# First expert layer of a fused attention and two-expert kernel: h of all tokens first, then y by seven products

## The chip, the core and the metric

One core of a Trainium2 chip. The metric is the device time of one launch in microseconds; the kernel before takes 979.49 us (median of three runs, 979.18 to 980.4). TensorE does matmuls into PSUM (eight banks of 512 float32 columns), VectorE, ScalarE and GpSimd work on elements, and all DMAs of this kernel are issued by SyncE's queue (SP).

## The reference

Everything is float32. Attention over 4 batches, 8 heads, 576 tokens, 64 channels, with a mask by blocks of 64 tokens; its output is 2304 tokens of 512 channels. Two expert layers follow:

```
x = attention(q, k, v)                      # scores only where block(query) >= block(key)
x = x.transpose(0, 2, 1, 3).reshape(2304, 512)
h = x @ moe_w_in                            # 512 x 2048
g = where(h >= 1, h, where(h <= -1, 0, (h + 1)**2 / 4))
x = g @ moe_w_out                           # 2048 x 512
h = x @ moe2_w_in
out = maximum(0.01 * h, h) @ moe2_w_out
```

The weights arrive as 64-bit floats; a conversion on the chip makes float32 of them.

## The kernel before

**Split operands.** Every operand of an expert matmul is split into a high and a low part that TensorE takes at full rate (float32r), and each product is three matmuls: high x high, low x high, high x low. One matmul contracts 128 rows and streams its columns past 128 loaded weight columns.

**Attention.** Sixteen pairs of heads, each in two units: `a` (tokens 0 to 319 of a batch) and `b` (320 to 575). A unit has scores (`unit_scores`, L555 for the plain form, L559 for the split one), softmax on VectorE, ScalarE and GpSimd (L466 to L486: maximum, exponential with sum, reciprocal, scaling of the probabilities on GpSimd), transposes on TensorE (L647), their copies out (L652, L654), values (L663), a split of the result (L676, L678) and a store to the DRAM tensor `x1d`. Its buffers are two "rooms" in the SBUF slots P1 and P2; it uses two PSUM slots of two banks, three for the first four units.

**First expert layer.** `moe_block` runs for blocks of tokens: five of 256, two of 512. For each pair of 128-row groups (`fc`) of w_in it makes h (L730), then on ScalarE and VectorE g and its two parts gh and gl (L738 to L744), and then at once the share of y (L761) that these rows of g give; y stays in two PSUM banks (four for the 512 blocks) until the block ends, and goes to the DRAM tensor `x2d` (L783). TensorE alternates h, y and attention. All of w_in and w_out of this layer lies in 16 SBUF tiles `w0` to `w15`.

**Conversions.** `w_float`, `w_hi` and `w_lo` convert the 32 halves of w1 at the start (L405 to L419, L374, L382). `conv_unit` converts w2 in 32 units and forms the seven combinations of weight blocks that the second layer takes (L810 to L823), and stores them to `wcd`; that runs beside the two 512 blocks.

**Second expert layer.** In two phases: h of all tokens (`h_step`, L937), stored to DRAM (`gd`), then y (`y_unit`, L1002) in units of 256 positions. Both use seven products in place of eight on matrices cut into 2x2 blocks (`PRODUCTS`, `ORDER`); tokens are paired as position (first half of a batch, second half). `sums` (L846, L848) adds the seven results up to four blocks, `w_load` brings the combined weights back and splits them (L833 to L835), `y_unit` loads g, forms its differences (L983) and splits them (L988 to L992).

**Order.** A planner (`Plan`) lists every operation with an engine, a cost, a priority and its reads and writes, simulates a list schedule in which each engine takes the waiting operation of lowest priority number, and emits the instructions in that order; each engine's queue on the chip then runs in that fixed order. The constants T_ and AHEAD set the priorities. A DMA counts as an operation of SP. Until the first h matmul, and between y matmuls of block 0, gaps of TensorE in the plan are filled with matmuls of zeros (`fill`).

Of the kernel before, what the change touches and what calls it, by code (L numbers as in the profile page):

```python
# [32 lines left out]
BLOCKS = [(256 * i, 256) for i in range(5)] + [(1280, 512), (1792, 512)]  # L33
# [11 lines left out]
W1_LO = ("dve", "pool")  # L45
W2_LO = ("dve", "pool")
T_MOE, T_FIRST, T_BLOCK, T_CONV = 30.0, 66.0, 66.0, 4.4
A1_LATE, A1_STEP, T_PACE = 0.0, 10.0, 2.4

AHEAD = 30.0  # L50
# [67 lines left out]
class Slot:  # L118
# [7 lines left out]
    def begin(self, dtype):  # L126
        self.n += 1
        n = self.n
        self.dtype = dtype
        self.live = []  # L130
        self.era = Buf(self.plan, ("slot", self.name), 1, lambda: self.pool.tile(
            [128, self.size], dtype, tag=self.name, name=f"{self.name}_{n}", bufs=1))
# [122 lines left out]
def fused_kernel(ctx, tc, qk, qk2, v, w1, w2, out):  # L255
# [84 lines left out]
    phase = {"late": False}  # L340

    def bank(i):

        ar = None if i in (4, 5) else ps_d if phase["late"] else ps_c
        return Bank(plan, (i,), lambda: banks[i], ar)

    def xbuf(i, tb):


        if tb < 384:  # L350
            where = ((A0, A1)[i % 2], 0), ((A0, A1)[i % 2], 1024)
        else:
            where = ((P1, 0), (P1, 2048)) if i == 5 else ((A0, 0), (A1, 0))
        for sl_ in dict.fromkeys(w[0] for w in where):
            sl_.begin(F32R)
        return [w[0].reg(w[1], NKC * tb, shape=lambda ap: ap.rearrange("p (k t) -> p k t", k=NKC)) for w in where], where[0][0]
# [11 lines left out]
    def w_tile(layer, fc):  # L368
        W[layer, fc] = pt(wp, [128, 2, 1024], F32R, f"w{fc}", f"w{layer}_{fc}", 1)

    def w_hi(prio, layer, fc, half, src, view, sb):
        t = W[layer, fc]
        s = slice(half * 512, half * 512 + 512)
        act(512, prio, lambda: nc.scalar.activation(t.get()[:, 0, s], view(), AF.Copy), [src],  # L374
            [(t, (half * 2, half * 2 + 1))], sb=sb)

    def w_lo(prio, layer, fc, half, src, view, sb, eng="dve"):
        t = W[layer, fc]
        s = slice(half * 512, half * 512 + 512)

        def f():
            (nc.vector if eng == "dve" else nc.gpsimd).tensor_tensor(  # L382
                t.get()[:, 1, s], view(), bc(t.get()[:, 0, s]), op=ALU.subtract)
        rw = [src, (t, (half * 2, half * 2 + 1))], [(t, (half * 2 + 1, half * 2 + 2))]
        if eng == "dve":
            dve(512, prio, f, *rw, port=sb)
        else:
            plan.op("POOL", 1225, prio, f, *rw, True)

    def w_float(prio, layer, fc, half, hs, keep=None, raw=None, sg=None):  # L390
# [3 lines left out]
        n = f"{layer}_{fc}_{half}"  # L394
        raw = raw or wraw()
        sg = sg or wsg()
        src = w1[fc, :, half * 1024:half * 1024 + 1024]
# [14 lines left out]
        part = None  # L412
        if keep is None:
            dst, view = hs, hs.get
        elif keep == "sg":
            dst, view = sg, sg.get
        else:
            dst, view, part = keep, lambda: keep.get()[:, half * 512:half * 512 + 512], (half, half + 1)
# [755 lines left out]
```

## Time and profile before

| | us |
|---|---|
| median of three runs | 979.49 |
| the profiled execution | 981.28 |
| span of its profile | 979.5 |
| TensorE busy | 959.4 (98%) |
| VectorE busy | 661.6 (68%) |
| ScalarE busy | 511.9 (52%) |
| GpSimd busy | 269.0 (27%) |
| DMA | 158.40 MB, mean 162 GB/s |

The span runs from the first to the last instruction of the program on the profiled execution; PE is TensorE's matmuls, PEld its weight loads, DVE VectorE, ACT ScalarE, POOL GpSimd, SPq SyncE's queue. The record of a matmul includes its way through the array, so that consecutive matmuls overlap: the price of one is taken from the length of a run in the chain of waits, divided by its count. The clock is TensorE's granted one as a share of 2.4 GHz. The DMA share is the mean busy share of the core's 16 DMA engines. The stages: attention and conversions until about 125 us, attention beside the 256 blocks until about 430, the 512 blocks until about 614, then the second layer's h until about 791 and its y until the end.

### The profile page before, as it was taken

Reading aid. Unit: us, or ns where it says so; the run is one execution under the profiler, and the core shown is the slowest. Engines: PE = TensorE matmul, PEld = TensorE weight load, DVE = VectorE, ACT = ScalarE, POOL = GpSimd, SP = SyncE. Lnnn points to the kernel's source line nnn. Section 1 sums busy time; section 2 is a strip of 40 time slices with the busy share of each in tenths; the row PEclk is TensorE's granted clock in tenths of the full one; section 3 lists DMA queues with packets and bytes.
Section 4 is the critical chain, followed back from the end, with each engine's and each line's share of the span. In section 5 each row is a group of like instructions: output and inputs, shape, how many; then the busy total and the mean of one; then the engine's idle time right before and its main releaser. Section 6 shows DMA issues by size and latency. Waiting matters only on the chain.

```text
span 979.5 us, 18953 instructions
## 1 busy us (share of the span) xinstructions
PE 959.4 (98%) x7040; PEld 878.5 (90%) x7040; DVE 661.6 (68%) x1229; ACT 511.9 (52%) x1064; POOL 269.0 (27%) x490
## 2 busy tenths in 40 slices
PE   8789999999999999999999999999999999999997
PEld 6578889889899899998888888999999999999997
DVE  4988855665655556545656754666757999988876
ACT  5677865666565566544444654342334654334332
POOL 6666533223241221336776410202020000000000
PEclk9999999999999999999999999999999999999999
DMA  7666542434425223488677732533434983443523
GB/s 242 196 213 216 177 161 74 158 96 130 150 84 157 84 73 106 130 273 293 224 261 242 284 104 76 189 119 134 136 122 146 302 279 105 144 137 116 148 80 109
DMA packets 113469, 158.40 MB, mean 162 GB/s; under 512 B 11232, under 2 KB 91104, under 8 KB 113376
## 3 DMA queue, kind: packets, MB, share of 16 engines
q1 hardware_dynamic: 113376, 157.19, 49.9%
q8 instruction: 55, 0.90, 0.4%
q14 instruction: 38, 0.31, 0.1%
HBM read 105.78 MB, written 51.38 MB: 160 GB/s over the span
## 4 chain that ended last, share of the span: by engine, by line
PE 91%; DVE 3%; ACT 2%; DMA 2%; issue 1%; POOL 0%; SPq 0%; DVEq 0%; ACTq 0%
PE bank L730 21%; PE bank L761 20%; PE bank L937 18%; PE bank L1002 17%; PE slot L647 5%; PE slot L663 5%; PE slot L559 2%; PE slot L555 2%; ACT rp L475 1%; DMA wraw<-w 1%; DMA gd<-ra 0%; DMA rg<-gd 0%; POOL rp L486 0%; DVE w L382 0%; DVE nmb L468 0%
## 5 line engine op out<-in xcount | busy, mean ns | idle before, releaser
L761 PE MATMUL bank<-rg,w 128*128 128x256 f32 (+1 forms) x1344 | 223.4, 316 | 0.0
L761 PEld LDWEIGHTS bank<-rg,w 128*128 128x128 f32 x1344 | 191.5, 188 | 21.6 <-issue 4.6
L730 PE MATMUL bank<-ra,w 128*128 128x256 f32 (+1 forms) x1152 | 180.7, 305 | 2.1 <-DVE rg L744 1.3
L937 PEld LDWEIGHTS bank<-rp,wc 128*128 128x128 f32 x1344 | 179.5, 189 | 1.0 <-ACT ra L848 0.7
L937 PE MATMUL bank<-rp,wc 128*128 128x288 f32 x1344 | 179.9, 296 | 0.5 <-ACT ra L848 0.5
L730 PEld LDWEIGHTS bank<-ra,w 128*128 128x128 f32 x1152 | 156.8, 189 | 17.9 <-issue 6.5
L1002 PE MATMUL bank<-wc,rp 128*128 128x256 f32 x1014 | 150.7, 282 | 0.8 <-DVE rp L990 0.8
L1002 PEld LDWEIGHTS bank<-wc,rp 128*128 128x128 f32 x1014 | 133.8, 188 | 1.0 <-DVE rp L990 1.0
L846 DVE TENSOR_TENSOR ra<-bank,ra 128x288 f32<-128x288 f32 (+2 forms) x203 | 93.1, 486 | 41.7 <-ACT ra L848 22.9
L741 DVE SCALAR_TENSOR_TENSOR bank<-bank,g 128x512 f32<-128x512 f32 x72 | 50.1, 696 | 69.4 <-ACT g L740 69.2
L738 ACT ACTIVATE g<-bank 128x512 f32<-128x512 f32 x72 | 42.9, 596 | 71.6 <-PE bank L730 71.4
L821 POOL TENSOR_TENSOR rp<-rp 128x128 f32<-128x128 f32 x128 | 67.5, 552 | 36.2 <-DVE rp L817 34.2
L486 POOL TENSOR_SCALAR rp<-rp,rsb 128x448 f32<-128x448 f32 (+1 forms) x64 | 47.7, 755 | 105.3 <-DVE rsb L481 100.5
L647 PE MATMUL slot<-ident,rp 128*128 128x128 f32 x480 | 64.8, 281 | 7.3 <-POOL rp L486 4.8
L744 DVE TENSOR_TENSOR rg<-bank,rg 128x512 fp32r<-128x512 f32 x72 | 49.5, 688 | 27.1 <-ACT rg L743 26.6
L743 ACT ACTIVATE rg<-bank 128x512 fp32r<-128x512 f32 x72 | 43.0, 597 | 41.1 <-DVE bank L741 41.1
L486 POOL TENSOR_SCALAR rp<-rp,rsa 64x64 f32<-64x64 f32 (+2 forms) x96 | 40.9, 441 | 85.7 <-DVE rsa L481 85.6
L647 PEld LDWEIGHTS slot<-ident,rp 128*128 128x128 f32 x480 | 55.2, 144 | 10.2 <-POOL rp L486 5.9
L989 ACT ACTIVATE rp<-ra 128x1024 fp32r<-128x1024 f32 (+1 forms) x39 | 37.8, 969 | 45.3 <-DVE ra L983 38.7
L1002 PE MATMUL bank<-wc,wraw 128*128 128x256 f32 x294 | 60.4, 282 | 0.2 <-DVE wraw L990 0.2
L941 ACT ACTIVATE ra<-ra 128x1152 f32<-128x1152 f32 x24 | 28.0, 1167 | 58.0 <-DVE ra L846 58.0
L663 PE MATMUL slot<-rp,rp 128*64 128x256 f32 (+2 forms) x512 | 57.2, 366 | 0.0
(122 smaller groups left out, 1424.2 us busy)
## 6 DMA issues: line engine op xcount, KB each, us to landing
wraw<-w SPq DMA_DIRECT2D x64, 256.0 KB, 3.7
wcd<-rp SPq DMA_DIRECT2D x32, 448.0 KB, 3.0
wc<-wcd SPq DMA_DIRECT2D x32, 448.0 KB, 4.2
gd<-ra SPq DMA_DIRECT2D x24, 576.0 KB, 3.6
wraw<-w SPq DMA_DIRECT2D x22, 512.0 KB, 4.2
rp<-qk SPq DMA_DIRECT2D x16, 416.0 KB, 3.2
rp<-gd SPq DMA_DIRECT2D x52, 128.0 KB, 2.9
rp<-gd SPq DMA_DIRECT2D x23, 256.0 KB, 3.2
```

The lines of the kernel that those rows point to most:

```text
L486: pool(keys, prio, lambda probs=probs, k=k, i=i, rows=rows: nc.gpsimd.tensor_scalar(probs[k]()[0:rows], probs[k]()[0:rows], rs.get()[0:row ...
L647: nc.tensor.transpose(s.get()[:, hd, o:o + 128], pr.get()[:, hd, a:a + 128], ident.get())
L663: nc.tensor.matmul(s.get()[64 * hd:64 * hd + 64, 0, q0:q0 + m], lhsT=vt.get()[:, j, 64 * hd:64 * hd + 64], rhs=pts[i].get()[:, hd, o:o + m ...
L730: nc.tensor.matmul(ps.get()[:, j * tb:(j + 1) * tb], lhsT=win(0, fc, p, kc), rhs=xt[x].get()[:, kc], start=(k == 0 and kc == 0 and j == 0) ...
L741: dve(nw, pv, lambda ps=ps, gt=gt: nc.vector.scalar_tensor_tensor(ps.get()[:, 0:nw], ps.get()[:, 0:nw], 1.0, gt.get()[:, 0:nw], op0=ALU.ma ...
L743: act(nw, pv, lambda ps=ps, gh=gh: nc.scalar.activation(gh.get()[:, 0:nw], ps.get()[:, 0:nw], AF.Copy), [ps], [gh])
L744: dve(nw, pv, lambda ps=ps, gh=gh, gl=gl: nc.vector.tensor_tensor(gl.get()[:, 0:nw], ps.get()[:, 0:nw], bc(gh.get()[:, 0:nw]), op=ALU.subt ...
L761: nc.tensor.matmul(y[o].get()[:, e * tb:(e + 1) * tb], lhsT=wout(0, fc, p)[:, ec * 128:ec * 128 + 128], rhs=x.get()[:, j * tb:(j + 1) * tb ...
L821: plan.op("POOL", 430, prio, lambda o=o, a=a, b=b, op=op: nc.gpsimd.tensor_tensor(sl(o), sl(a), sl(b), op=op), [(fx, (a, a + 1)), (fx, (b, ...
L846: dve(cols, prio, lambda: nc.vector.tensor_tensor(out(o), P[b][1](), out(a), op=ALU.add), [P[b][0], (slots, (a, a + 1))], [(slots, (o, o + ...
L937: nc.tensor.matmul(ps.get()[:, 0:HALF], lhsT=wc(0, p, cw, li, 128 * kc, 128 * kc + 128), rhs=r.get()[:, cx, kc], start=(k == 0 and kc == 0 ...
L1002: nc.tensor.matmul(ps.get()[:, 256 * t:256 * t + 256], lhsT=x.get()[:, n * zi + 128 * t:n * zi + 128 * t + 128], rhs=wc(1, p, cw, li, 0, 2 ...
```

## The change

The first layer gets the form of the second. `h1_block` makes h and g of nine blocks of 256 tokens, beside the attention, and stores g to DRAM (`gd[0]`); `y_unit` is made general and makes y of all positions after that, with seven products, in units of 232 positions (the last has 224) where the weights are the loaded operand and g streams. Positions now pair the tokens of two blocks of 256 (`runs`), within the first block two halves of 128. Only w_in of w1 is converted at the start (`w_float`, sixteen times, into `w0` to `w7`); w_out of w1 goes through `conv_unit` into `wcd`, as w2 does, and the conversion of w2's second half moves into the second layer's h. The tiles `w8` to `w15` are free until y begins, and hold three more rooms for the attention, the raw words of `w_float`, and the buffers of the 32 conversions that run beside the attention. The attention has three PSUM slots throughout (banks 0 to 3, 6 and 7; h has 4 and 5), and up to two units of scores ahead of the values. The order of its units is written out, b and a of the next batch in turn, and `NEED` says how many units precede each block. The filler ends with the first h matmul.

```diff
-BLOCKS = [(256 * i, 256) for i in range(5)] + [(1280, 512), (1792, 512)]
+NBLK = 9
...
-T_MOE, T_FIRST, T_BLOCK, T_CONV = 30.0, 66.0, 66.0, 4.4
-A1_LATE, A1_STEP, T_PACE = 0.0, 10.0, 2.4
-
-AHEAD = 30.0
+SQUARE = ("act",)
+T_MOE, T_FIRST, T_BLOCK, T_CONV = 30.0, 50.0, 41.0, 2.8
+T_UNIT = 10.2
+DEPTH = 2
+T_W2, T_NEXT = 100.0, 7.0
+
+AHEAD = 45.0
...
+    C = {i: Slot(plan, wp, f"w{i}", 1792) for i in range(8, NFC)}
...
+    ROOMS = {0: {"p": [(P1, 0)], "v": (P2, 1536), "qk": (P2, 2560)},
+             1: {"p": [(P2, 0)], "v": (P2, 2176), "qk": (P2, 3392)},
+             2: {"p": [(C[8], 0), (C[9], 0)], "v": (C[8], 1152), "qk": (C[10], 0)},
+             3: {"p": [(C[11], 0)], "v": (C[12], 0), "qk": (C[12], 384)},
+             4: {"p": [(C[13], 0), (C[14], 0)], "v": (C[13], 1152), "qk": (C[15], 0)}}
...
+    def h1_block(i, p0, dp, hbanks):
+
+        xt = XB[i]
+        for p in range(NP2):
...
+                for k, (c, x) in enumerate(((0, 0), (1, 0), (0, 1))):
+                    def f(fc=fc, j=j, k=k, c=c, x=x, ps=ps):
+                        plan.fill = None
+                        for kc in range(NKC):
+                            nc.tensor.matmul(ps.get()[:, j * 256:(j + 1) * 256], lhsT=win(fc, c, kc),
+                                             rhs=xt[x].get()[:, kc], start=(k == 0 and kc == 0 and j == 0),
+                                             stop=(k == 2 and kc == NKC - 1), skip_group_check=True)
+                    pe(4 * 119.5, pr + 0.01 * j, f, [(W[p], (2 * c + j, 2 * c + j + 1)), xt[x]], [ps])
+            gt = G2.reg(turn("g1", (0, 512, 1024, 1536)), 512)
+            pv = pr - 8
+            act(512, pv, lambda ps=ps, gt=gt: nc.scalar.activation(gt.get(), ps.get(), AF.Relu, bias=0.5, scale=0.5), [ps], [gt])
...
+                act(512, pv, lambda gt=gt: nc.scalar.activation(gt.get(), gt.get(), AF.Square), [gt], [gt], sb=True)
+            dve(512, pv, lambda ps=ps, gt=gt: nc.vector.scalar_tensor_tensor(
+                gt.get(), ps.get(), 1.0, gt.get(), op0=ALU.max, op1=ALU.min), [ps, gt], [gt])
...
+            dma(262144, pv + 1, lambda src=src, dst=dst: nc.sync.dma_start(dst, src()), [gt], where)
...
     def h_step(b, p, pr, dp, banks_):
-        h = (turn("h", (A0, A1, G2)) if b < B - 1 else (A1, A0)[p % 2]).reg(0, 1152, shape=lambda ap: ap.rearrange("p (s t) -> p s t", s=4))
+        h = (A1, A0)[p % 2].reg(0, 1152, shape=lambda ap: ap.rearrange("p (s t) -> p s t", s=4))
...
                     def f(k=k, cw=cw, x=x[0] if isinstance(x, tuple) else x, ps=ps, li=li, zi=zi, p=p):
                         for t in range(nt):
-                            nc.tensor.matmul(ps.get()[:, 256 * t:256 * t + 256],
-                                             lhsT=x.get()[:, n * zi + 128 * t:n * zi + 128 * t + 128],
-                                             rhs=wc(1, p, cw, li, 0, 256), start=(p == 0 and k == 0 and t == 0),
-                                             stop=(p == NP2 - 1 and k == 2), skip_group_check=True)
+                            a, e = (0, n) if wide else (128 * t, 128 * t + 128)
+                            b = wc(z, p, cw, li, 128 * t, 128 * t + 128) if wide else wc(z, p, cw, li, 0, 256)
+                            g = x.get()[:, n * zi + a:n * zi + e]
+                            nc.tensor.matmul(ps.get()[:, 256 * t:256 * t + w], lhsT=b if wide else g, rhs=g if wide else b,
+                                             start=(p == 0 and k == 0 and t == 0), stop=(p == NP2 - 1 and k == 2), skip_group_check=True)
...
+    order = [u for p in range(NP) for u in ((p, "b", (0, 4)[p % 2]), (NP + p, "a", 1))]
     for b in range(1, B):
         for p in range(NP):
+            order.append((NP * b + p, "b", (0, 2)[p % 2]))
             if b + 1 < B:
+                order.append((NP * (b + 1) + p, "a", (1, 3)[p % 2]))
+    seq = [(p, "a", (1, 0, 4, 1)[p], 4.0 * p) for p in range(NP)] + [(*u, T_MOE - AHEAD + T_UNIT * i) for i, u in enumerate(order)]
+    ring = [0, 3, 1]
...
+    NEED = [0, 7, 8, 15, 16, 23, 24, 24, 28]
+    for i in range(NBLK):
+        dp = (T_FIRST if i == 0 else T_BLOCK if i < NBLK - 1 else 24.0) / NFC
...
+        h1_block(i, t, dp, hb)
         t += dp * NFC
     for i in range(32):
+        conv(i // 16, i % 16, T_W2 + T_NEXT * i)
...
+    for p in range(NP2):
+        w_load(0, p, t - 60 + 6 * p, t - 40 + 5 * p)
+    pos = 0
+    while pos < NPOS:
+        n = min(232, NPOS - pos)
+        dp = 4.7
+        y_unit(0, pos, n, t, dp, every)
+        if pos + n == NPOS:
+            h_first(t + 8, t + 20)
+            for p in range(NP2):
+                w_load(1, p, t + dp * p, t + dp * p + 10)
+        t += dp * NP2
+        pos += n
...
             h_step(b, p, t + dp * p, dp, every)
+            if b < B - 1 and p < 6:
+                conv(2, 6 * b + p, t + dp * p) if 6 * b + p < 16 else None
             if b == B - 1:
-                w_load(1, p, t + dp * p, t + dp * p + 10)
+                w_load(2, p, t + dp * p, t + dp * p + 10)
```


## Rows read from the trace of the kernel before

**Rows 1.** The page's chain of waits: share of the span by line.

```profile
PE bank L730 21%; PE bank L761 20%; PE bank L937 18%; PE bank L1002 17%; PE slot L647 5%; PE slot L663 5%; PE slot L559 2%; PE slot L555 2%; ACT rp L475 1%; DMA wraw<-w 1%; DMA gd<-ra 0%; DMA rg<-gd 0%; POOL rp L486 0%; DVE w L382 0%; DVE nmb L468 0%
```

**Rows 2.** Windows by stage: length, busy time of each engine (count), clock, DMA.

```profile
0.00:125.00 125.00, 110.80 (x847) 93.54 (x848) 99.75 (x189) 88.65 (x229) 77.58 (x134) 0.97 0.65 212
125.00:430.00 305.00, 305.00 (x2525) 276.01 (x2524) 174.16 (x355) 181.18 (x495) 87.70 (x200) 1.00 0.39 121
430.00:611.00 181.00, 181.00 (x805) 147.76 (x804) 106.48 (x145) 94.37 (x151) 85.02 (x144) 1.00 0.65 218
611.00:791.00 180.00, 179.50 (x1337) 178.69 (x1336) 125.66 (x261) 73.27 (x102) 18.68 (x12) 1.00 0.50 167
791.00:973.00 182.00, 181.02 (x1519) 180.60 (x1519) 152.99 (x274) 74.05 (x90) 0.00 (x0) 1.00 0.46 137
```

**Rows 3.** Windows, four stretches from 25 to 125: their sum.

```profile
sum 100.00, PE 90.67 PEld 76.88 DVE 87.15 ACT 74.71 POOL 62.16; mean PE 22.67 PEld 19.22 DVE 21.79 ACT 18.68 POOL 15.54
```

**Rows 4.** Chain of waits in order of time: start, length, what (count).

```profile
112.10 2.10 PE slot L663 x20
...
127.66 1.34 PE slot L663 x12
...
180.25 2.10 PE slot L663 x20
...
290.01 1.75 PE slot L647 x16
...
415.85 2.10 PE slot L663 x20
...
449.65 2.79 PE bank L730 x12
...
612.99 2.10 PE bank L761 x9
...
621.02 169.06 PE bank L937 x1266
...
800.73 158.70 PE bank L1002 x1335
```

**Rows 5.** Windows of L730 alone, then of L761: PE, PEld, clock, DMA.

```profile
0.00:125.00 125.00, 27.23 (x192) 24.36 (x192) 0.97 0.65 212
...
0.00:125.00 125.00, 22.27 (x168) 20.64 (x168) 0.97 0.65 212
```

**Rows 6.** DMA issues: tiles, count, size of one, median time to landing.

```profile
wraw<-w SPq DMA_DIRECT2D x64, 256.0 KB, 3.7
...
wcd<-rp SPq DMA_DIRECT2D x32, 448.0 KB, 3.0
...
x1d<-rp SPq DMA_DIRECT2D x16, 256.0 KB, 3.0
...
ra<-x1d SPq DMA_DIRECT2D x8, 512.0 KB, 4.6
```

**Rows 7.** Windows of L409, of L419, of L382: VectorE (and GpSimd), clock, DMA.

```profile
0.00:126.00 126.00, 26.18 (x32) 0.97 0.65 213
...
0.00:126.00 126.00, 22.00 (x32) 0.97 0.65 213
...
0.00:126.00 126.00, 10.89 (x16) 20.38 (x16) 0.97 0.65 213
```

**Rows 8.** Groups by line: busy time, mean ns of one, idle before.

```profile
L814 DVE SCALAR_TENSOR_TENSOR rp<-wraw,rp 128x512 int32<-128x512 int32 x32 | 23.9, 747 | 11.7 <-POOL rp L812 9.9 <-DMA wraw<-w 1.8
...
L835 DVE TENSOR_TENSOR wc<-wc,wc 128x896 fp32r<-128x896 f32 x32 | 34.2, 1097 | 3.3 <-ACT wc L834 3.2
```

**Rows 9.** Windows of two stretches with much DMA, columns as in rows 2.

```profile
450.00:525.00 75.00, 75.00 (x324) 60.80 (x323) 45.53 (x65) 34.43 (x57) 51.43 (x92) 1.00 0.76 259
...
775.00:800.00 25.00, 25.00 (x194) 25.00 (x194) 22.89 (x45) 15.82 (x19) 0.00 (x0) 1.00 0.93 307
```

**Rows 10.** The tile wsg: one operation, ns min/median/max, first and last start.

```profile
L409 DVE SCALAR_TENSOR_TENSOR wsg<-wraw,wsg x10: 656/692/2959, 10.9 to 120.4; 128x512 int32<-128x512 int32 x10
```

More of the change, by code (lines that the diff above doesn't have):

```diff
@@ L366, in fused_kernel, with w_float @@
     W = {}
[L368 to L397, printed above, removed]
+    def w_float(prio, fc):
+        raw, sg = (C[8 + fc % 5].reg(z, m) for z, m in ((0, 1024), (1024, 512)))
+        hs = bank(5)
+        src = w1[fc, :, 0:1024]
+        t, j = W[fc // 2], fc % 2
+        s = slice(512 * j, 512 * j + 512)
         def words():
@@ L630, in unit_values @@
         n = f"{part}{pair}"
-        vt, pr = units[pair, part]
+        vt, pr, prob = units[pair, part]
         pts = []
@@ new lines, in moe_load, with runs @@
+            dma(512 * tb * 4, prio, lambda c=c: nc.sync.dma_start(bc(x[c].get()), x1d[:, c, :, t0:t0 + tb]),
+                [(f"x1d{k}", (t0, t0 + tb)) for k in range(NKC)], [x[c]])
+    def runs(pos0, n):
+        out_ = []
+        while n:
+            if pos0 < 128:
+                m, t0, d = min(n, 128 - pos0), pos0, 128
+            else:
+                i, q = divmod(pos0 - 128, 256)
+                m, t0, d = min(n, 256 - q), 256 + 512 * i + q, 256
+            out_.append((pos0, m, t0, d))
+            pos0, n = pos0 + m, n - m
+        return out_
@@ L1040, in fused_kernel, with attention @@
+    ring = [0, 3, 1]
     rooms = {}
-    def attention(units):
-        last = None
+    queue = []
+    def attention(units, flush=False):
         for pair, part, room, t in units:
-            ring = wide if (pair < NP and part == "a") else two
-            if last is not None and rooms[last[:2]] == room:
-                unit_values(*last)
-                last = None
+            while queue and (len(queue) >= DEPTH or any(rooms[u[:2]] == room for u in queue)):
+                unit_values(*queue.pop(0))
@@ L1050, in attention, with conv @@
             unit_scores(pair, part, t - 5, ring, room)
-            if last is not None:
-                unit_values(*last)
             rooms[pair, part] = room
-            last = pair, part, t - 4, ring, EVAC[part]
-        unit_values(*last)
+            queue.append((pair, part, t - 4, ring, EVAC[part]))
+        while queue and flush:
+            unit_values(*queue.pop(0))
+    def conv(z, i, prio):
+        p, s = divmod(i, 2)
+        if z < 2:
+            c = C[(14, 15)[i % 2]]
+            bufs = c.reg(0, 1024), C[13].reg(896 * (i % 2), 896), c.reg(1024, 512)
+        else:
+            bufs = wraw(), G2.reg(896 * (i % 2), 896), wsg()
+        conv_unit(z, p, s, prio, *bufs)
```

384 lines of the change are left out of this document (145 added, 239 removed).

## Prediction

> **What bounds the kernel now.** I read the chain of waits first: four matmul lines carry 76% of the span, h and y of the first expert layer (L730, L761), then h and y of the second (L937, L1002) [rows 1]. Then the busy times by stage [rows 2]. From 125 to 613 TensorE has no idle time at all, in the second layer it lacks 0.5 and 1.0 us, and only the first 125 us have slack: 110.8 busy, filler matmuls included. VectorE is at 57 to 84% later on, and at 87% from 25 to 125 [rows 3], where it converts the first weights. So the kernel is a sum of matmuls behind a start that VectorE limits, and two things can move it: the matmul time, and the start.
>
> The prices of a matmul come from long runs of the chain [rows 4]: 2.79/12 = 232.5 ns for 512 columns, 169.06/1266 = 133.5 for 288, 158.70/1335 = 118.9 for 256, and a 128-column transpose, which loads 128 new weight columns for 128 streamed ones, 1.75/16 = 109.
>
> **Check of the method on before.** The first layer is 1920 matmuls of 256 and 768 of 512 columns: 228.3 + 178.6 = 406.9 us. 360 of the 256 ones lie before 125 [rows 5]. Its last long row ends at 615.1 [rows 4], a dozen matmuls of the second layer (1.6) ahead of it: call its end 613.5. From 125 on: 488.5 less 1560 x 0.1189 + 178.6 = 364.1 leaves 124.4 for 12 pairs of attention, one half unit already done: 10.6 us of TensorE a pair (units a and b), gaps included. Split as 12 to 18 transposes and as 1.34 to 2.10 of values [rows 4], a unit b is 6.4, a unit a 4.2. The second layer is 1344 x 0.1335 = 179.4 and 1512 x 0.1189 = 179.8; 613.5 + 179.4 + 179.8 = 972.7, so tail and small gaps are 6.8 of the 979.5.
>
> **The change, part by part.**
>
> *y by seven products.* Removed: 203.4 (half of 406.9). Added: four units of 232 and one of 224 positions, each 8 x 7 x 3 x 2 = 336 matmuls. Neither width is in the trace. The line through 256 and 512 is 0.444 ns a column: 108.3 and 104.7 ns, so 1344 x 0.1083 + 336 x 0.1047 = 180.8. Below, the slope from 256 to 288 (0.456) gives 107.9: 180.0. Above, no gain at all from narrowing: 1680 x 0.1189 = 199.8. The weight-load floor that the transposes show (109) would give 183.1. I take 180.8; the nearest row, 256, is only 24 columns away. Its VectorE work is that of the second layer's y per column, where VectorE is at 84% [rows 2] and TensorE full. Gain 22.6.
>
> *h of all tokens.* All blocks are 256 wide now: 1728 x 0.1189 = 205.5 instead of 203.4, loss 2.1. Each step loses the copy to gh, the subtraction to gl and the chain behind them, and gains a 256 KB store on the SP queue; in the trace a store of that size lands in 3.0 us [rows 6] and four tiles of gt cover that. Below and above: 0 and 3 us for one late store at the end.
>
> *The start.* Converting w1 costs VectorE 26.2 + 22.0 + 10.9 = 59.1 us before 126 [rows 7]; only w_in, half of it, is left there: -29.5. But block 1 now needs seven units (four b, three a, order written out), where before the fourth b had its values at 114.2 [rows 4] with hardly an a begun. From 125 to 430 VectorE had 174.2 us [rows 2] for 12 pairs and 32.5 steps of the layer (1560/48) with two 512-column operations each, like the 0.747 us of L814 [rows 8]: (174.2 - 48.6)/12 = 10.5 a pair, two fifths for a unit a: three are +12.6. Net -17, at 87% busy -19: 95. Then the x1d store and the load of the block, 3.0 + 4.6 [rows 6]: block 1 can start at 103, with block 0 and eight units done. Bounds: 90 (the a units ride free) and 122 (the saving buys nothing, and the granted clock, 0.97 of 2.4 GHz on average in this stage [rows 2], so for some us at 1.2, is lower as the filler now ends with the first h matmul).
>
> *From 103 on.* TensorE has 8 blocks x 192 x 0.1189 = 182.6 and 20 units, 8 x 10.6 + 4 x 6.4 = 110.4: 293.0 us. Is it fed? Two blocks need four pairs: 42.4 + 45.7 = 88.1, a pair every 22.0 us. Before, twelve b units had their values between 180.25 and 415.85 [rows 4]: a pair every 21.4, on two PSUM slots and two rooms. It now has three slots and five rooms, so the attention's own pace suffices; the last four units have blocks 5 to 7 (68.5 us) beside them. Price 0 below; above, see the rivals.
>
> *The moved conversions.* 32 conversions (16 for w_out of w1, 16 for w2), each with three DMAs, one ScalarE, two VectorE and five GpSimd operations, now run beside the attention; those of 430 to 611 held GpSimd for 85.0 us [rows 2], which beside 62 for its own work there (87.7 x 8.5/12) is half of 293. On VectorE 32 x 2 x 0.747 = 48 [rows 8]; with 116 (8/12 of the 174.2), 25 for four more b units, 16 for 21 more steps and 18 of weight loads that is 223 of 293 us, 76%. On the DMA queue it is tighter: conversions 32 x (2 x 0.262 + 0.459) MB = 31.5 [rows 6], first weight load 7.3, g stores 64 x 0.262 = 16.8, attention and x some 32 (estimate: 121 GB/s x 305 us = 36.9 [rows 2], less four a units and the x2d stores): 88 MB, 300 GB/s. At full share the stages show 121/0.39 = 310 to 218/0.65 = 335 GB/s [rows 2]: 92 to 97% of the queue. Free if late transfers are only conversions (below: 0); above: the 259 GB/s of 450 to 525 [rows 9], 340 us, +47. I take +6, near the low end, because 25 us at 307 GB/s and share 0.93 went by without TensorE idle [rows 9] and a third of the bytes may wait.
>
> The Trainium skill (DMA: Bandwidth & Descriptors, Specifications) puts a core's HBM limit at about 358 GB/s. By it the 88 MB would take 246 us, 84% of the stretch, the +6 would go and the sum be 953; no stage here shows such a rate.
>
> *Seams.* Into y: its first operands (g of blocks 0 to 2) are old, rooms are free once the attention ends, so only buffer hand-over: 0 to 8, take 3. From y to the second h: the weights wc for it can only be loaded as the last y unit leaves their tiles, 16 x 1.097 = 17.6 of VectorE [rows 8]; in its 35 us and the 45 of the next h batch VectorE has 0.84 x 35 + 17.6 + (125.7 - 17.6)/4 [rows 2] + 6 conversions x 1.49 = 83: just over. 0 to 27 (none of the weights and conversions hidden), take 3 at the seam and 4 in h. Last stage unchanged: 179.8 and 6.8.
>
> **Sum.** 103 + 293.0 + 6 + 3 + 180.8 + 3 + 179.4 + 4 + 179.8 + 6.8 = 958.8 for the span of 979.5. The profiled execution's own time was 981.28, 1.8 more than its span; so 960.6 against 981.28, which is -20.7, and 979.49 - 20.7 = 959 against the median of the runs. In gains: y 22.6, start 15, lost again h 2, DMA 6, seams 10.
>
> **Rivals.**
> (A) *Narrow matmuls cost what 256 columns cost.* For it: no row lies between 128 and 256 columns. Against it: 128 columns with a fresh weight load take 109, less than 118.9. Time 959 + 19 = 978.
> (B) *The DMA queue decides the attention stage; slower.* Place: 103 to 396. SP issues in one order, so a store that waits for its producer holds the loads of the next unit behind it, and the attention's loads of q and k stand behind 0.5 MB conversions. For it: 300 GB/s asked over 293 us, more than any stage of rows 2 moved. Against it: the 307 GB/s stretch. At 259 GB/s: 340 us, so 959 - 6 + 47 = 1000. It makes the kernel slower from 88 MB/321 us = 274 GB/s downwards.
> (C) *VectorE and GpSimd get in each other's way.* The conversions bring 32 GpSimd units into the stage where GpSimd also scales the probabilities, as in 25 to 125, where GpSimd was 62% and VectorE 87% busy and TensorE 90.7% with its fillers [rows 3]. One VectorE operation with two SBUF inputs took 2959 ns there against a median of 692 [rows 10]. If 293 us of matmuls run at that 90.7%, they take 323: 959 + 30 = 989. Against it: VectorE stays under 80%. Slower from 93% downwards.
> The Trainium skill (SBUF — State Buffer, Who interferes with whom) says that a VectorE instruction with two SBUF inputs and a GpSimd instruction that reads SBUF exclude each other for the whole instruction; the 2959 ns agree with that. By that rule (C) is the outcome if the conversions' pieces fall into the softmax.
> (D) *The start gains nothing* (122 instead of 103): 978. For it: the first four a units and their rooms are latency, not VectorE work.
>
> **How the numbers follow.** Forecast 60%, own range 944 to 972 (start 90 to 112, DMA 0 to 12, seams 3 to 15). A 4%, D 9%, B 14%, C 6%; better than 944 by several low bounds together 7%. A difference under 0.2% (2 us) can't be told from none. Slower: B and C without their mild part, 18%. Within 0.2%: part of A and D, 5%. Faster: 77%. Range: from 940 up to 988; B's and some of C's weight lies above.
>
> **What would show it.** Right: h matmuls solid from about 103 to 400, VectorE under 85% there; the y matmuls of L1002's successor 108 ns apart and their stage 181 to 184 us; second layer as before. Wrong: matmul groups that wait on a load of q, k or x (B) or on the probabilities' scaling (C) between 100 and 400; 119 ns spacing at 232 columns (A); block 1 later than 115 (D); waits on sums in the first 45 us of the second h.

## The result, and the profile after

| | before | after |
|---|---|---|
| median on the same chip, us | 979.34 (four runs, 978.41 to 980.40) | 955.22 (four runs, 955.19 to 957.39) |
| ratio | | 0.9759, 95% interval 0.9742 to 0.9776 |
| profiled execution, us | 981.28 | 957.39 |
| its span, us | 979.5 | 955.6 |

The change takes 24.1 us, 2.4%. The profiled execution is the longest of the four (the spans of the others are 953.4); all readings of after below are from it. In the new file L715 is the first layer's h, L966 y of both layers, L887 the second layer's h, L638 the attention's transposes, L654 its values.

The chain of waits of after, shares of the span by line, answers to [rows 1]; the four matmul lines have become three and carry 74% of it, where they carried 76%.

```profile
PE bank L966 37%; PE bank L715 19%; PE bank L887 18%; PE slot L654 5%; PE slot L638 5%; PE slot L548 2%; PE slot L544 2%; DVE ra L795 1%; DMA w<-w 1%; DMA x1d<-rp 1%; DMA rp<-gd 1%; DMA rp<-qk 0%; DVE wc L784 0%; ACT rp L449 0%; DMA rp<-v 0%
```

The windows of after by stage answer to [rows 2] (length, busy time of PE, PEld, DVE, ACT, POOL with counts, clock, DMA share, GB/s): the start, the blocks beside the attention, the first y, the second h, the second y.

```profile
0.00:104.00 104.00, 96.59 (x742) 74.33 (x744) 80.48 (x178) 80.00 (x248) 73.58 (x192) 1.00 0.76 236
104.00:398.00 294.00, 291.51 (x2420) 267.20 (x2419) 214.05 (x401) 208.33 (x508) 157.34 (x339) 1.00 0.87 287
398.00:584.00 186.00, 185.20 (x1654) 185.01 (x1653) 152.37 (x264) 82.92 (x103) 4.40 (x3) 1.00 0.55 158
584.00:770.00 186.00, 185.15 (x1393) 184.44 (x1392) 161.28 (x312) 90.56 (x127) 62.44 (x93) 1.00 0.78 259
770.00:951.00 181.00, 180.15 (x1515) 179.77 (x1513) 153.83 (x276) 71.84 (x87) 0.00 (x0) 1.00 0.44 132
```

What to see: the stage beside the attention has only 2.5 us of 294 without a matmul, and VectorE is at 73% there; the three stages after 398 lack 0.8, 0.85 and 0.85 us. The DMA moved 287 GB/s over that stage, 84 MB, at a share of 0.87. The clock is 1.00 in the start, where it was 0.97.

The chain of after in order of time (start, length, what) answers to [rows 4].

```profile
402.52 145.03 PE bank L966 x1296
557.73 31.75 PE bank L966 x282
...
777.20 171.73 PE bank L966 x1444
```

The price of a y matmul is in the first row: 145.03/1296 = 111.9 ns in the units of 232 columns, where I had 108.3; the 256 columns of the last stage are at 171.73/1444 = 118.9, as before. The end of the first h is not quite 402.5: 18 matmuls of the first y lie before it, so h alone ends at 400.5. The 1444 are not the whole last stage either: all 1512 matmuls of the second y lie between 770.2 and 951.1.

The second h begins at 589.48, right behind the last matmul of y; the window of that stage above has TensorE busy for all but 0.85 us.

```profile
574.96 14.52 PE bank L966 x130
589.48 12.02 PE bank L887 x90
```

### The profile page after: what moved, and what is told of

Its sections match the earlier page's. It is cut to its first block, busy times and chain, and to the rows that moved or that the text cites. A ratio compares the mean times of both kernels' runs of the same rounds, so it can differ in the third digit from the quotient of the medians.

```text
span 955.6 us, 21203 instructions
## 1 busy us (share of the span) xinstructions
PE 938.7 (98%) x7714; PEld 890.8 (93%) x7714; DVE 763.1 (80%) x1431; ACT 533.7 (56%) x1068; POOL 297.8 (31%) x626
## 4 chain that ended last, share of the span: by engine, by line
PE 87%; DVE 5%; DMA 4%; ACT 2%; issue 1%; POOL 1%; SPq 0%; DVEq 0%; POOLq 0%; ACTq 0%
PE bank L966 37%; PE bank L715 19%; PE bank L887 18%; PE slot L654 5%; PE slot L638 5%; PE slot L548 2%; PE slot L544 2%; DVE ra L795 1%; DMA w<-w 1%; DMA x1d<-rp 1%; DMA rp<-gd 1%; DMA rp<-qk 0%; DVE wc L784 0%; ACT rp L449 0%; DMA rp<-v 0%
## 5 line engine op out<-in xcount | busy, mean ns | idle before, releaser
L715 PE MATMUL bank<-ra,wi 128*128 128x256 f32 x1728 | 227.8, 286 | 1.6 <-DVE rg L726 1.5
L715 PEld LDWEIGHTS bank<-ra,wi 128*128 128x128 f32 x1728 | 211.8, 188 | 11.0 <-issue 4.9
L887 PE MATMUL bank<-rp,wc 128*128 128x288 f32 x1344 | 180.2, 296 | 0.8 <-DVE ra L795 0.7
L887 PEld LDWEIGHTS bank<-rp,wc 128*128 128x128 f32 x1344 | 179.4, 189 | 1.6 <-DVE ra L795 0.9
L795 DVE TENSOR_TENSOR ra<-bank,ra 128x288 f32<-128x288 f32 (+4 forms) x294 | 132.6, 493 | 30.0 <-PE bank L966 13.3
L966 PE MATMUL bank<-wc,rp 128*128 128x256 f32 x1014 | 151.5, 282 | 0.0
L966 PEld LDWEIGHTS bank<-wc,rp 128*128 128x128 f32 x1014 | 134.2, 188 | 0.0
L966 PE MATMUL bank<-rp,wc 128*128 128x232 f32 (+1 forms) x952 | 127.9, 275 | 0.0
L966 PEld LDWEIGHTS bank<-rp,wc 128*128 128x128 f32 x952 | 117.1, 192 | 0.0
L950 ACT ACTIVATE rp<-ra 128x1024 fp32r<-128x1024 f32 (+2 forms) x61 | 59.3, 972 | 73.6 <-DVE ra L944 66.5
L769 POOL TENSOR_TENSOR w<-w 128x128 f32<-128x128 f32 x128 | 65.5, 532 | 43.9 <-DVE w L765 39.2
L949 ACT ACTIVATE rp<-rp 128x696 fp32r<-128x696 f32 (+3 forms) x49 | 38.0, 776 | 70.8 <-PE bank L966 64.8
L953 DVE TENSOR_TENSOR wraw<-ra,rp 128x1024 fp32r<-128x1024 f32 (+2 forms) x61 | 68.2, 1117 | 5.1 <-PE bank L966 2.1
L966 PE MATMUL bank<-rg,wc 128*128 128x232 f32 (+1 forms) x408 | 61.7, 275 | 0.8 <-ACT rg L950 0.8
L784 DVE TENSOR_TENSOR wc<-wc,wc 128x896 fp32r<-128x896 f32 x48 | 53.9, 1132 | 10.6 <-ACT wc L783 10.3
L966 PE MATMUL bank<-wc,wraw 128*128 128x256 f32 x294 | 61.1, 282 | 0.8 <-DVE wraw L951 0.8
L966 PE MATMUL bank<-wraw,wc 128*128 128x232 f32 (+1 forms) x320 | 61.1, 275 | 0.0
L721 ACT ACTIVATE rg<-bank 128x512 f32<-128x512 f32 x72 | 43.2, 600 | 31.6 <-PE bank L715 28.0
```

The costliest lines, as they stand in the source:

```text
L715: nc.tensor.matmul(ps.get()[:, j * 256:(j + 1) * 256], lhsT=win(fc, c, kc), rhs=xt[x].get()[:, kc], start=(k == 0 and kc == 0 and j == 0), ...
L769: plan.op("POOL", 430, prio, lambda o=o, a=a, b=b, op=op: nc.gpsimd.tensor_tensor(sl(o), sl(a), sl(b), op=op), [(fx, (a, a + 1)), (fx, (b, ...
L784: dve(896, late, lambda s=s: nc.vector.tensor_tensor(view(lo, s), bc(view(lo, s)), bc(view(hi, s)), op=ALU.subtract), [(lo, part), (hi, pa ...
L795: dve(cols, prio, lambda: nc.vector.tensor_tensor(out(o), P[b][1](), out(a), op=ALU.add), [P[b][0], (slots, (a, a + 1))], [(slots, (o, o + ...
L887: nc.tensor.matmul(ps.get()[:, 0:HALF], lhsT=wc(1, p, cw, li, 128 * kc, 128 * kc + 128), rhs=r.get()[:, cx, kc], start=(k == 0 and kc == 0 ...
L950: act(4 * n, pv, lambda tt=tt, ht=ht: nc.scalar.activation(s_(ht, 0, 4), s_(tt, 0, 4), AF.Copy), [tt], [ht], sb=True)
```

## The forecast's sum against the trace

Ends of stages by the rows above and by the timeline (start, length, what): the last matmuls of block 0, the first of block 1, the first and the last of the second y.

```profile
104.26 1.69 PE L715 MATMUL bank<-ra,wi 128*128 128x256 f32 x12
...
111.20 0.71 PE L715 MATMUL bank<-ra,wi 128*128 128x256 f32 x4
...
770.20 1.60 PE L966 MATMUL bank<-wc,rg 128*128 128x256 f32 x12
...
950.78 0.28 PE L966 MATMUL bank<-wc,rp 128*128 128x256 f32 x1
```

| term | forecast | after | from |
|---|---|---|---|
| start, to block 1 | 103 | 111.2 | its first matmul; block 0's last ends at 105.9 |
| blocks 1 to 8 with 20 units, DMA | 293.0 + 6 | 289.3 | 400.5 - 111.2 |
| seam, y of the first layer, seam | 3 + 180.8 + 3 | 189.0 | 589.5 - 400.5; 1680 x 0.1118 = 187.8 of it y |
| second h | 179.4 + 4 | 180.7 | 770.2 - 589.5 |
| second y | 179.8 | 180.9 | 951.1 - 770.2 |
| tail (in the forecast with small gaps) | 6.8 | 4.5 | 955.6 - 951.1 |
| span | 958.8 | 955.6 | |

Between block 0's end and block 1's start TensorE has the values of the eighth unit and pieces of the next units; some of the stage's work is thus done before 111.2, and the first two rows taken together are 400.5 for 402.

The misses oppose one another: the matmuls of y took 7.0 more than forecast, the start 8.2 and the second y 1.1, while the stage took 9.7 less, the two seams 4.8 of the 6 set aside less, the second h 2.7 and the tail 2.3. Whether each term was right for the reason given is what the experiments are for. All are made from the changed kernel; times are medians, ratios are to the kernel before on the same chip. A difference to after is one of medians from different chips, where the kernel before took 978.5 to 980.3 us, and after's trace is of an execution 2.2 us above its median: such a difference is good to some 2 us, and the traces give it up to 3 us smaller. Where stages are compared I take the first and last matmuls of their lines in the traces.

## Experiments

**1. Is the y matmul held by a floor? Units of 192, then of 256.** The 111.8 ns of 232 columns can be the forecast line, 0.444 ns a column, off by a little, or a floor that no narrower unit gets under.

```
e1:  n = min(192, NPOS - pos)       # 6 units
e2:  n = min(256, NPOS - pos)       # 4 units and one of 128
```

> The first layer's y in six units of 192 positions instead of four of 232 and one of 224 (2016 matmuls instead of 1680). Theory: a matmul that needs a new load of 128 weight columns cannot come faster than about 111.8 ns (the pace at 232 and at 224 columns in the changed kernel), so 2016 x 0.1118 = 225.4 against 187.8: +37.6, about 993. Rival: the 111.8 is only the stream of 232 columns with a larger fixed part, and 192 columns would come at 118.9 less 64 x 0.444 = 90.5 ns: 2016 x 0.0905 = 182.4, about 950; spacing of the matmuls near 90 instead of 112 ns.

> The first layer's y in four units of 256 positions and one of 128 (again 1680 matmuls). Theory (floor of 111.8 ns a matmul): 1344 x 0.1189 + 336 x 0.1118 = 197.4 against 187.8: +9.6, about 965, and the unit of 128 at 112 ns a matmul. Rival (columns alone): 159.8 + 336 x 0.062 = 180.6, -7, about 948.

Measured: 1002.5 us (1.0226, 1.0192 to 1.0259) and 970.9 us (0.9904, 0.988 to 0.9929). The windows of y at 232 columns in after and at 192 in e1, then in e2 those of the 128 unit and of the seam behind it (columns as above):

```profile
450.00:475.00 25.00, 25.00 (x226) 25.00 (x225) 18.45 (x34) 9.38 (x12) 0.00 (x0) 1.00 0.40 108
```

```profile
450.00:475.00 25.00, 25.00 (x226) 25.00 (x226) 15.56 (x31) 7.21 (x10) 0.00 (x0) 1.00 0.29 80
```

```profile
563.00:588.00 25.00, 25.00 (x227) 25.00 (x225) 16.63 (x40) 10.05 (x17) 0.00 (x0) 1.00 0.79 257
600.00:625.00 25.00, 22.13 (x149) 21.04 (x148) 25.00 (x39) 11.96 (x17) 12.09 (x11) 0.93 0.88 281
```

25 us hold 226 matmuls at 232 columns, 226 at 192 and 227 at 128: the floor holds from 232 columns down to 128. (A window also counts the matmuls that are under way at its start, and the record of one is 0.275 us long, so 226 are 25.275/226 = 111.8 ns, as in the chain; 227 are 111.3.)

Both kernels lost somewhat more than the floor explains. From the last h matmul of the first layer to the first matmul of the second y after takes 367.7 us, e1 409.3 (405.6 to 814.9) and e2 380.6 (402.6 to 783.2). e1's y is 2016 x 0.1118 = 225.4 for 187.8, 37.6 of its 41.6; e2's is 1344 x 0.1189 + 336 x 0.1113 = 197.2, 9.4 of its 12.9. In e2 the rest, 3.5, stands for the most part in the last row: VectorE is busy 25.00 of 25 us at the hand-over to the second h, TensorE lacks 2.9 and the clock falls to 0.93. That the last unit of y hides the second h's weights, and no longer does when it is shorter, fits the two runs, which lose 4.0 and 3.5 us beyond the floor, and was not tested by itself. That was the seam that I had priced at 0 to 27.

**2. What the floor belongs to: weight columns, rows, or the matmul.** From e1, with half of the weight columns, then half of the rows of contraction, in all matmuls of the first y but the first of each product (1932 of the 2016); both kernels leave out half of y's sums.

```
e10:  matmul(ps[0:64, ...], lhsT=b[:, 0:64], rhs=g)
e11:  matmul(ps[...], lhsT=b[0:64], rhs=g[0:64])
```

> As e1_y192 (six units of 192 positions, 1002.5 us, about 111 ns a matmul), but all matmuls of y of the first layer after the first of each product load only 64 of the 128 weight columns and write 64 of the 128 PSUM partitions: half of y's sums are left out, the instructions and their streamed columns stay. Theory (the floor is the load of 128 weight columns, and goes with the number of weight columns): the matmuls of y come at their streaming pace, near 90 ns (192/232 of 108.3 ns), 25 us has some 260 to 280 of them, and the run falls to 960 to 970 us unless VectorE then paces y. Rival 1 (a fixed price of each matmul, whatever it loads): 225 per 25 us as before, 1000 to 1004 us. Rival 2 (the load goes with the rows, not the columns): as rival 1 here, but e11 falls.

> As e1_y192, but all matmuls of y of the first layer after the first of each product use 64 of the 128 rows of contraction, of the weights and of g: half of y's sums are left out, 128 weight columns of 64 rows are loaded, 192 columns stream as before. If the floor goes with the weight columns or is a fixed price of a matmul: 225 per 25 us, 1000 to 1004 us. If it goes with the rows that a weight load writes: near 90 ns, 260 to 280 matmuls in 25 us, 960 to 970 us.

Measured: 959.9 us for e10 (0.9805, 0.9775 to 0.9834), 1220.2 us for e11 (1.2464, 1.2425 to 1.2503). The windows of e10, then of e11, each over y:

```profile
450.00:475.00 25.00, 25.00 (x282) 25.00 (x281) 21.60 (x47) 10.04 (x14) 0.00 (x0) 1.00 0.53 148
```

```profile
450.00:475.00 25.00, 25.00 (x113) 24.15 (x112) 9.09 (x19) 4.01 (x6) 0.00 (x0) 0.50 0.24 69
```

```profile
417.04 354.01 PE bank L967 x1594
```

The weight loads of y in e1, e10 and e11 (busy us, mean ns of one):

```profile
L966 PEld LDWEIGHTS bank<-rp,wc 128*128 128x128 f32 x1140 | 140.3, 192 | 0.7 <-ACT rp L949 0.7
```

```profile
L967 PEld LDWEIGHTS bank<-rp,wc 128*64 128x64 f32 x1092 | 104.9, 135 | 0.8 <-DVE rp L951 0.8
```

```profile
L967 PEld LDWEIGHTS bank<-rp,wc 64*128 64x128 f32 x1092 | 249.2, 326 | 4.0 <-issue 2.9 <-DVE ra L944 0.2
```

With 64 weight columns and the same 192 streamed ones, 282 matmuls fit: 89.5 ns, near the 90.5 that e1's expectation gives for streaming 192 columns, and the run is 42.6 us shorter (1932 x (111.8 - 89.5) = 43). So the floor goes with the 128 weight columns; rival 1 is out. e10 also writes half of the PSUM partitions, but the record of the weight load itself went from 192 to 135 ns. e11 was answered in a way that no theory expected: the granted clock fell to 0.50, 1.2 of 2.4 GHz, as y began, with TensorE at 25.00 of 25 us, and was back at 0.99 over the second h; in e10, with all rows and half of the columns, every 25 us from 425 to 700 show 1.00. The chain of e11 (third fence) gives 354.01/1594 = 222.1 ns, 1.99 times the 111.8, and more than the 179 that streaming would take at half the clock (2 x 89.5): half the rows buy nothing, so the floor does not go with the rows.

The Trainium skill (TensorE: Matmul & The Clock Gate, LDWEIGHTS) says that a weight load takes time by its columns and not by its rows; e10 and e11 agree. Its figure for 128 columns, about 107 ns, lies under the 108.3 of streaming 232, by which y would have cost the forecast 180.8; measured is 111.8, and the measurement decides.

**3. Was the start paced by VectorE? More of its work there.** The first bit operation of each conversion of w_in is made three times: the same result, 32 more operations (0.68 us each, 22 us) on VectorE in the start.

```
+        for _ in range(3):
             dve(512, prio, ...)      # words >> 29 | sg, of w_float
```

> Each of the 16 conversions at the start makes its first bit operation on VectorE three times instead of once (the result does not change): 32 operations of 0.72 us, 23 us more of VectorE before about 80 us, near to what the change took away there. Theory (VectorE sets the length of the start): block 1 starts 15 to 25 us later, 970 to 980. Rival (the start is latency of the first units, and the gain came from the third room and PSUM): +0 to +5, 955 to 960.

Measured: 974.6 us (0.9945, 0.993 to 0.9961), 19.4 more than after. The window of the start:

```profile
0.00:104.00 104.00, 92.25 (x674) 69.23 (x675) 89.39 (x183) 69.86 (x224) 69.17 (x169) 0.97 0.65 207
```

68 fewer matmuls are done at 104 than in after, and block 1 begins at 127.2 for 111.2: 16 of the 22 us of VectorE came out as time in the start. So VectorE's work there is time of the start, as I had said. The way is another than in the sum, which moved the fourth unit b: that has its values only 6.1 us later (104.8 for 98.7). What ends late is block 0 (127.4 for 105.9), for whose matmuls the weights are converted. That the conversion of w_out did to the start of before just what this work does here is likely and was not run.

**4. Do rooms and PSUM slots matter?** I had given them no price in the sum: by my reading the attention's pace of before sufficed on two slots and two rooms.

```
e3:  every b unit in room 0, every a unit in room 1
e4:  if len(queue) and pair >= NP and len(ring) > 2:
         ring.remove(1)
```

> The attention with rooms 0 and 1 only, as before the change; all else as changed. Theory: from 104 us on TensorE is the bound and the attention kept a pair every 21.4 us with two rooms in the kernel before, so only the start loses, where the third unit waits for the first: +0 to +8, 955 to 963. Rival: with conversions and fuller queues beside it the attention needs the rooms; at 25 us a pair instead of 22 the stage grows by 8 x 3 = 24, 975 to 985, and matmuls of h wait for x.

> Two PSUM slots for the attention after its first four units, as before the change; the five rooms stay. Theory: TensorE stays the bound, +0 to +5, 955 to 960. Rival: the third slot is what hides the longer queues on VectorE and ScalarE; without it the scores wait for the copies of the transposes, +15 to +30, 970 to 985.

Measured: 974.8 us (0.9948, 0.9926 to 0.997), +19.6, with two rooms, and 991.6 us (1.0114, 1.0081 to 1.0147), +36.3, with two slots: that kernel is slower than before. The windows of the start and of the attention stage, of e3 and then of e4:

```profile
0.00:104.00 104.00, 87.97 (x632) 67.02 (x632) 77.48 (x163) 73.90 (x220) 78.36 (x180) 0.95 0.77 246
104.00:398.00 294.00, 289.02 (x2394) 262.57 (x2393) 206.91 (x389) 203.28 (x517) 160.83 (x350) 1.00 0.82 269
```

```profile
0.00:104.00 104.00, 88.84 (x638) 68.08 (x638) 71.36 (x152) 69.32 (x213) 63.97 (x169) 0.97 0.68 213
104.00:398.00 294.00, 276.48 (x2234) 244.61 (x2233) 205.48 (x392) 199.92 (x511) 161.79 (x361) 0.99 0.85 276
```

Follow the values of the b units. In e3, then in after (chains in order of time):

```profile
132.56 2.10 PE slot L654 x20
...
286.57 2.10 PE slot L654 x20
```

```profile
98.80 2.10 PE slot L654 x20
117.14 2.10 PE slot L654 x20
...
203.33 2.10 PE slot L654 x20
...
268.97 2.10 PE slot L654 x20
```

In e3 these are the fifth and the twelfth b unit, in after the fourth, fifth, ninth and twelfth: 154.0/7 = 22.0 us a pair with two rooms, 151.8/7 = 21.7 in after. In the long stage the rooms are not needed; the lag, 15 us at the fifth unit and 18 at the twelfth, was there when the stage began, and block 1 begins at 127.6 for 111.2. It is the start that needs them, as my theory for e3 had it, at twice the 8 us that it allowed. With two slots the start lags as well (block 1 at 131.7), and then the pace too is short. The timeline of e4 (start, length, what) has its fourth and its ninth b unit:

```profile
119.88 2.17 PE L654 MATMUL slot<-rp,w 128*64 128x256 f32 x20
...
232.62 2.17 PE L654 MATMUL slot<-rp,rp 128*64 128x256 f32 x20
```

That is 112.7/5 = 22.5 us a pair, against 20.9 in after for the same five ((203.33 - 98.80)/5), and 21 us late already at the fourth. TensorE's waits in e4 name the place, the transposes of the probabilities behind the exponentials (waiting group, what it waited for: us, times, longest); the last line is of after:

```profile
PE slot L638 <- ACT rp L449: 10.6, 6, 2.7
...
PE slot L638 <- ACT w L449: 3.3, 2, 2.2
```

```profile
PE slot L638 <- ACT rp L449: 0.5, 1, 0.5
```

So the new rooms and the third slot are parts of the gain. e4 keeps after's order and its two units of scores ahead, so it prices the slot in this kernel, not in the one before.

What was wrong is my reading of the pace of before, 21.4 us a pair. The last unit a there is at 360.86, so the last three of the eleven steps between 180.25 and 415.85 hold a unit b alone:

```profile
360.86 1.34 PE slot L663 x12
367.28 2.10 PE slot L663 x20
```

With a unit a in each step it was (367.28 - 180.25)/8 = 23.4 us a pair, slower than the 22.0 that the forecast needed, and with TensorE full all along, so that these rows never showed what the attention could keep on two slots. For the same eight steps after took 22.0.

**5. Is the DMA queue near its limit (rival B)?** The converted weights are stored twice.

```
+        if z < 2:
+            dma(458752, prio + 4, lambda: nc.sync.dma_start(wcx[z, p, s], fx.get()), ...)
```

> The 32 stores of converted weights beside the attention are each made a second time, into a DRAM tensor that nobody reads: 14.7 MB more in the stage from 104 to 398, which moves 287 GB/s x 294 us = 84 MB at a DMA share of 0.87. Theory: the queue has about an eighth left (38 us), the copies need 14.7 MB / 0.325 = 45 us of it: +0 to +10, 955 to 965. Rival (the DMA queue already sets the pace of the stage): +14.7 MB / 0.287 to / 0.325, +45 to +51, 1000 to 1006, with TensorE idle all along the stage.

Measured: 963.9 us (0.9835, 0.9807 to 0.9864), +8.7 for 14.7 MB. Window of the stage:

```profile
104.00:398.00 294.00, 287.96 (x2363) 263.32 (x2362) 204.78 (x383) 202.98 (x499) 151.88 (x338) 0.99 0.97 328
```

The queue carried 328 GB/s at share 0.97 and TensorE did 57 matmuls fewer in the stage. Rival B, that such a rate can't be had here, is refuted; the margin that the change left is small, an eighth of the 328 GB/s. The best stretch in after itself, the 25 us from 350, shows the same top, with TensorE 0.62 us short (it answers to [rows 9]):

```profile
350.00:375.00 25.00, 24.38 (x204) 24.06 (x203) 12.25 (x18) 15.36 (x25) 7.26 (x15) 1.00 0.99 335
```

**6. How much room has GpSimd (rival C)?** The squares of g move from ScalarE to GpSimd.

```
-SQUARE = ("act",)
+SQUARE = ("pool",)
```

> The square of every h step runs on GpSimd (some 1.3 us each, 72 of them) instead of ScalarE. GpSimd would be busy for some 157 + 83 = 240 of the 294 us from 104 to 398, and for longer when VectorE's operations with two SBUF inputs hold the port. Theory (TensorE is the bound, the other engines have room): +0 to +5, 955 to 960. Rival (VectorE and GpSimd are close to holding the attention up): the scaling of probabilities queues behind squares, +20 to +30, 975 to 985.

Measured: 1001.2 us (1.0215, 1.0185 to 1.0245), +46. The attention stage's window, a wait of TensorE, and three groups by line (busy us, mean ns of one):

```profile
104.00:398.00 294.00, 274.89 (x2217) 247.20 (x2214) 205.91 (x370) 163.19 (x434) 218.13 (x390) 0.98 0.81 263
```

```profile
PE bank L715 <- DVE rg L726: 12.9, 12, 2.6
```

```profile
L723 POOL TENSOR_TENSOR rg<-rg 128x512 f32<-128x512 f32 x72 | 82.2, 1143 | 63.7 <-ACT rg L721 55.1 <-DMA wcd<-w 5.3 <-ACT rsb L453 2.3
...
L765 DVE SCALAR_TENSOR_TENSOR w<-w,w 128x512 int32<-128x512 int32 x32 | 28.5, 891 | 0.5
...
L762 DVE SCALAR_TENSOR_TENSOR w<-w,w 128x512 int32<-128x512 int32 x32 | 26.3, 822 | 9.7 <-POOL w L760 9.3 <-DMA gd<-rg 0.3
```

The same wait and groups in after:

```profile
PE bank L715 <- DVE rg L726: 1.5, 3, 0.6
```

```profile
L725 ACT ACTIVATE rg<-rg 128x512 f32<-128x512 f32 x72 | 45.7, 635 | 1.2
...
L765 DVE SCALAR_TENSOR_TENSOR w<-w,w 128x512 int32<-128x512 int32 x32 | 22.7, 709 | 0.8
L762 DVE SCALAR_TENSOR_TENSOR w<-w,w 128x512 int32<-128x512 int32 x32 | 21.8, 682 | 7.4 <-POOL w L760 5.9 <-DMA wraw<-qk 1.5
```

A square takes 1143 ns on GpSimd for 635 on ScalarE, and stands between h's matmuls and the release of their bank, of which h has two. TensorE's wait for that release went from 1.5 (the line of after above) to 12.9 us. Of the 43.2 us between the two traces 12.2 are lost before block 1 (123.4 for 111.2) and 28.6 from there to the last h matmul. VectorE's conversions became longer where GpSimd is busier, 709 to 891 and 682 to 822 ns, 20 to 26%. That is what rival C described, and the run has the longer chain besides: in after GpSimd is busy for 54% of this stage (157 of 294) and TensorE lacks 2.5 us, in e6 for 74% and TensorE lacks 19.1. I had expected 0 to 5 us and was wrong; the 46 were not split between the longer chain and the longer operations.

**7. A version without the floor.** Positions 0 to 127 are computed in the second layer's form: g is the loaded operand and 256 columns of weights stream, 168 matmuls for 336; its four outputs are turned by eight transposes within the next unit. The other 1024 positions are four units of 256.

```
-        n = min(232, NPOS - pos)
+    for pos, n in ((128, 256), (0, 128), (384, 256), (640, 256), (896, 256)):   # e8
+    for pos, n in ((0, 128), (128, 256), (384, 256), (640, 256), (896, 256)):   # e9
...
+        if layer == 0 and not wide:
+            yn = A0.reg(0, 1024, ...)
+            sums(p1, 256, yn, P, lambda o: yn.get()[:, o])
+            ... nc.tensor.transpose(ps[...], yn.get()[:, o, 128 * t:128 * t + 128], ident)
```

> A version meant to keep y of the first layer off the floor of about 111.8 ns that e1 and e2 showed for a matmul with its own fresh 128-column weight load. Positions 128-383 go first (256 columns, weights as the loaded operand), then positions 0-127 in the form of the second layer (g as the loaded operand, 256 columns of weights streaming: 168 matmuls in place of 336), whose four outputs are turned by 8 transposes in the middle of the next unit, then three units of 256. Theory (the floor is the whole excess of y): 1344 x 118.9 = 159.8, plus 168 x 118.9 = 20.0, plus 8 transposes and their wait at some 1 to 2 us, 181 to 182 in place of 187.8: 948 to 951 us. Rival (what is saved is lost again at the seams: the unit of 20 us leaves VectorE and ScalarE too little time to prepare weights and operands, or the last unit ends later for the second h, as in e2): 953 to 960 us, with the matrix engine idle over 3 us in the 50 us around the narrow unit or at the seam into the second h.

> As e8_y_turned, with the narrow unit (positions 0-127, 20 us) before all others, so that the weights of all eight pairs are needed within 20 us at the end of the attention stage. Theory (the preparation of weights paces that stretch, at 8 pairs of 4 instructions of 896 columns): 2 to 8 us slower than e8. Rival (the weights are prepared early enough): within 1 us of e8.

Measured: e8 949.4 us (0.9708, 0.969 to 0.9726), the fastest of all kernels here; its interval lies wholly below that of after (0.9742 to 0.9776), the ratio of the two is 0.9948. e9 952.6 us (0.9737, 0.9717 to 0.9757). The chain of e8 in order of time:

```profile
402.83 57.45 PE bank L966 x484
...
600.67 162.25 PE bank L887 x1212
762.92 177.44 PE bank L966 x1494
```

57.45/484 = 118.7 ns a matmul in the first y, which begins where after's does; from the last h matmul of the first layer to the first of the second y e8 takes 359.9 us (402.8 to 762.75), 7.8 less than after. The floor accounts for 187.8 - (1512 x 0.1189 + 8 x 0.109) = 7.1 of that, the last term the eight transposes. By the spans e8 is 8.6 shorter, by the medians 5.9. The last unit has 256 positions, and the second h lost nothing here.

In e9 the narrow unit comes first, and the first y is 3.3 us longer than in e8. The window where it begins has 2.7 of them:

```profile
400.00:425.00 25.00, 22.34 (x189) 22.14 (x188) 19.35 (x45) 14.54 (x24) 0.00 (x0) 1.00 0.58 179
```

```profile
PE bank L966 <- ACT rg L949: 2.7, 1, 2.7
```

It is one wait, for the high part of g that ScalarE makes (L949). In the 4 us before, ScalarE spends 1.8 on high parts of weights (L783) and waits 1.0 for loads of g, so the weights of my theory are a part of it and not all.

## Why the prediction was right, and where it was not

The forecast of 959 with -20.7 for the profiled execution met 955.2 and -23.9; the likeliest case came, and its own range (944 to 972) holds the time.

That the sum came out within 3.2 us of the span is luck in part: 7.0 us too little for the matmuls of y, 8.2 for the start and 1.1 for the second y stand against 19.5 too much in the other terms.

- *y by seven products:* right as a mechanism, the term was mis-sized. 180.8 for 187.8. The line through 256 and 512 columns was carried 24 columns down, across a floor; the bound that I had worked out from the transposes (109 ns, 183.1) was the right kind of answer and still 2.8 ns low, which no run explains. The transposes' 109 lay above the 108.3 that I took; I used the row only against the 118.9 of rival A. The sign that I had named for this term, 108 ns apart and a stage of 181 to 184, did not come: 111.8 and 189.0 with its seams.
- *The start:* 103 for 111.2. I moved the end of the fourth unit b from 114.2 to 95; it came at 100.9, and block 1 10.3 after it, not 7.6. That VectorE's work is time of the start held when work was put back (e7, 16 us for 22), by way of block 0's weights and not of the fourth b. That the start would be possible at all rested on the rooms and slots (e3, e4: 14 to 21 us late by the fourth b unit), which the text did not price. The granted clock did not fall with the earlier end of the filler: 1.00 for 0.97.
- *The attention stage:* it was fed, as forecast, with TensorE lacking 2.5 us from 104 to 398. The reason given, a pace of 21.4 us a pair on two slots and two rooms, was a misreading (23.4 with a unit a in each step). On two rooms the stage keeps its pace after the start (22.0 for 21.7 us a pair), on two slots it does not.
- *DMA:* +6 forecast, at most the 2.5 us without a matmul came. 84 MB moved for an estimate of 88, 287 GB/s for the 300 asked. B is refuted as a limit at this load (e5), with an eighth of the queue left. By the 310 to 335 GB/s of the text its 300 would have been 90 to 97% of the queue, not 92 to 97.
- *Seams:* 10 set aside; 1.2 came at the two seams and 1.3 in the second h. e1 and e2 lose 4.0 and 3.5 us beyond the floor when the last unit of y is shorter; the 224 positions of it were long enough.
- *Rivals A, C, D:* A named the right term with too high a price (119 ns, +19; 111.8 and +7 came). What C describes is seen in e6, where GpSimd is busy for 74% of the stage; at after's 54% the stage has 2.5 us without a matmul. D, block 1 at 122, did not come: 111.2, short of the 115 that I had named as its sign, but 8 of its 19 us did.

Left open: how e6 divides between the longer release of h's bank and the longer VectorE operations, what let the clock fall in e11, and why the floor lies 3 ns above the transposes' price.

## What to carry to other kernels

A line through matmul prices must not be carried below the price of its weight load: look for the narrowest matmul that loads new weights, and when a shape falls under it, exchange the operands so that the wide one streams (e8). A pace averaged over unlike units, beside a TensorE that is full, is no proof that its buffers suffice, above all not for the stage that fills the pipeline: take one slot away on the chip before calling more of them free (e4, e3). And where the last unit of a stage gives the next one's loading its time, shortening it can cost at the seam behind it (e2, 3.5 us).

## What was not expected of the hardware

- With half of the rows of contraction in use TensorE's granted clock fell to 0.50 while it was busy without a gap, and y at 192 columns went from 111.8 to 222.1 ns a matmul; with half of the weight columns it stayed at 1.00 (e11, e10).
- A matmul with a new 128-column weight load costs 111.3 to 111.9 ns at 128, 192 and 232 columns alike (e2, e1, after), and 89.5 at 192 with a 64-column load (e10).
- The DMA queue held 328 GB/s over 294 us at share 0.97 (e5), above every stage of [rows 2].
